# Window attention and a gated MLP on one core: 64-wide TensorE tiles for the attention, units of six blocks, and a transpose split between VectorE and DMA

## The chip, the core and the metric

The kernel runs on one core of one Trainium2 chip. A core has five engines with a queue each: TensorE (PE, matmuls; PEld is its weight load), VectorE (DVE), ScalarE (ACT), GpSimd (POOL) and SyncE (SP, which here only issues DMAs). Each engine takes its instructions in order and waits on semaphores for what other engines and the DMAs have made. The metric is the device time of one execution in microseconds (us); lower is better. The kernel before takes 1037.87 us (median of three runs, 1037.74 to 1038.93).

## The reference

`q`, `k`, `v` are (8 batches, 8 heads, 576 tokens, 64) in float32. Attention is causal with a window of 64 keys, its output becomes 4608 rows of 512, and these go through an MLP of width 2048 with a gate:

```
scores = q @ k.T / 8                     # masked unless 0 <= query - key < 64
attn   = softmax(scores)                 # over at most 64 keys
x      = (attn @ v) as [4608, 512]       # 8 heads side by side
h      = x @ w_in                        # [4608, 2048]
g      = h * tanh(log1p(exp(min(h, 20))))   # h itself instead of the logarithm above 20
out    = g @ w_out                       # [4608, 512]
```

The two weight matrices are handed to the chip as float64 bits; the kernel splits each into a high and a low float32r part there.

## The kernel before, in words

**Layout.** Heads go in four pairs, so that a pair fills 128 partitions (two heads of 64 channels). Tokens go in 12 chunks of 384, a chunk in six blocks of 64 queries. A block of queries sees two blocks of keys, its own and the one ahead of it, hence 128 keys. There are 288 such (pair, block) items in all, 24 a chunk.

**Attention of one block** (L126 to L173), in groups of three blocks. `q_t` holds the two heads of a pair apart in the columns, with zeros across the heads, so one 128x128x128 float32 matmul (L126) gives both heads' scores `s_ps`. VectorE adds the mask and takes the row minimum of the negated scores (L131). ScalarE takes the exponential and its row sum (L135). VectorE adds 1e-9 and inverts the sum (L137, L138). GpSimd multiplies the rows by it for the first three chunks; later VectorE does two blocks of three (L143) and GpSimd one (L141). The product `pr` has queries on partitions and must be transposed to `pT`, keys on partitions. Chunks 0 and 1 do that with TensorE (L157) and a ScalarE copy (L158). From chunk 2 on VectorE does it in 32x32 squares (L153): ten instructions a group, of 32x96 each, without the squares that the mask empties. Then `o_ps` is one 128x128x128 float32 matmul a block (L165), of which only the two diagonal quarters are used: ScalarE rounds them to float32r as `xh` (L172), VectorE takes the rest as `xl` (L173). Each float32 matmul is two LDWEIGHTS and two MATMUL records in the trace.

**MLP of one chunk**: 16 steps `f`. A step is twelve matmuls of 384 columns into `h_ps` (L181: three products of high and low parts, four slices of 128 channels), then the gate, and nine matmuls of 512 columns into three accumulators `acc` (L211). The gate is exp on ScalarE (L188), a clip on VectorE (L193), square, logarithm and exp on ScalarE (L194 to L196), a product on VectorE (L198), and the split in `gh` and `gl` on GpSimd (L199, L200). The matmuls into `acc` run two steps behind those into `h_ps` (`LAG`). Where no attention runs beside (`alone`), ScalarE first copies `h_ps` to `h` (L192).

**Weights.** 32 pieces of 512 columns are loaded once and split by bit operations (`load_w`, L225 to L245): four or five VectorE instructions a piece (L236 to L243), ScalarE rounds (L244), and VectorE or GpSimd subtracts (L245). `take_w(2)` asks for two pieces a step.

**Order of the work.** First the attention of chunks 0 and 1, with eight pieces of weights between. Then a segment `both` of 24 steps: all 16 of chunk 1 and the first eight of chunk 0, while the other pieces are split. Then the last eight steps of chunk 0 beside the attention of chunk 2. From there on chunk c's 16 steps stand beside the attention of chunk c+1; chunk 11 has none beside it. `Att.plan` gives each group's three stages (scores, transpose, values) a slot among the half steps. A scheduler then fixes each engine's order; a tile is taken from a pool with a fixed number of buffers, in the program's order, and an instruction that needs a buffer waits for whoever last used it. Before the change the gate's `t` has four buffers of its own, and the split's `wa` has two of its own.

Of the kernel before, what the change touches and what calls it, by code (L numbers as in the profile page):

```python
# [19 lines left out]
BLK = 64          # the attention window; queries and keys go in blocks of it  # L20
# [3 lines left out]
WP = 512          # columns of weights taken at a time  # L24
# [3 lines left out]
def tile_window_attn_mish_ffn(  # L28
    ctx: ExitStack,
    tc: tile.TileContext,  # L30
    q2: bass.AP,      # [pairs, 128 (head of the pair, d), blocks x (head, 64 queries)], zero across heads
    kT: bass.AP,      # [pairs, 128, 64 + tokens]
    vN: bass.AP,      # [pairs, 64 + tokens, 128]
    w_in: bass.AP,    # [f tiles, 128, c tiles, 128], the doubles' bits
    w_out: bass.AP,   # [f tiles, 128, 512], the doubles' bits
    out: bass.AP,     # [tokens, 512]
# [3 lines left out]
    NPAIR, _, NT = q2.shape  # L40
    NT //= 2
# [6 lines left out]
    G = 3                       # blocks of an attention group  # L48
    NG = NB // G
# [16 lines left out]
    mask0 = const.tile([P, P], F32, name="mask0")  # L66
# [7 lines left out]
    nc.gpsimd.tensor_copy(mask0, mask)  # L74
    nc.gpsimd.memset(mask0[:, 0:BLK], NEG)

# [5 lines left out]
    pTs = [const.tile([P, G, P], F32, name=f"pT{i}") for i in range(2)]  # L82
# [4 lines left out]
    marks = {}        # the last of VectorE's instructions on a group's scores  # L87

    def load_qk(c, p):
        q_t = ap_.tile([P, NB, P], F32, name="q_t")  # L90
        k_t = ap_.tile([P, CH + BLK], F32, name="k_t", bufs=2)
        qf = q_t.rearrange("p n s -> p (n s)")
        parts = NG if c == 0 and p < 2 else 1
        for i in range(parts):
            a, b = i * CH // parts, (i + 1) * CH // parts
            nc.sync.dma_start(qf[:, 2 * a:2 * b], q2[p, :, 2 * (c * CH + a):2 * (c * CH + b)])
            a, b = a + BLK * (i > 0), b + BLK
            nc.sync.dma_start(k_t[:, a:b], kT[p, :, c * CH + a:c * CH + b])
# [10 lines left out]
    def att_scores(c, i, tiles):  # L109
        p, g = units[i]  # L110
        q_t, k_t = tiles
        if c < 2:
            n = i % NTT
            s_ps = ps_acc.tile([P, G, P], F32, name="s_ps", tag=f"acc{n}")
        else:
            s_ps = ps_at.tile([P, G, P], F32, name="s_ps", tag="at")
        if c < 2 and i % 2 == 0:
            # the tiles of the gate, which has not begun
            pr = mp.tile([P, CH], F32, name="prt", tag="t", bufs=4).rearrange("p (g s) -> p g s", g=G)
        else:  # L120
            pr = ap_.tile([P, G, P], F32, name="pr", bufs=3)
        mx = ap_.tile([P, G], F32, name="mx", bufs=5)
        sm = ap_.tile([P, G], F32, name="sm", bufs=5)
        for j in range(G):
            n = g * G + j
            nc.tensor.matmul(s_ps[:, j, :], q_t[:, n, :], k_t[:, n * BLK:n * BLK + P],  # L126
                             start=True, stop=True)
        for j in range(G):
            first = (c * NB + g * G + j) % blocks_per_seq == 0
            # -(scores + mask) / 8 and its minimum, which is minus the maximum  # L130
            marks[c, i] = nc.vector.tensor_tensor_reduce(  # L131
# [283 lines left out]
```

## Time and profile before

| what | value |
|---|---|
| runs | 1037.87, 1038.93, 1037.74 us |
| profiled execution: span | 1039.1 us (its time outside the span is not recorded apart) |
| mean granted TensorE clock | 0.982 |
| busy: PE / PEld / DVE / ACT / POOL | 979.3 / 877.7 / 796.2 / 625.8 / 398.9 us |
| end of the attention of chunks 0 and 1, first gate on DVE | 63.1 us |
| chunk 1's first result leaves on DVE | 186.6 us |
| chunk 2's first full step on PE | 249.7 us |
| a chunk from 3 to 9 | 80 us each |
| DMA | 76.05 MB, 73 GB/s over the span |

PE's busy time is near the span, but matmul ends are modelled and a waiting matmul counts as busy, so PE is read by the starts of its instructions: the distance from one start to the next. The stages differ, so they are read one by one.

### The profile page before, as it was taken

How to read it: one execution, taken by the hardware profiler on the slowest of the kernel's cores; microseconds unless marked ns; L12 is line 12 of the kernel's file. 1: busy time of each engine (PE TensorE's matmuls, PEld its weight loads, DVE VectorE, ACT ScalarE, POOL GpSimd, SP SyncE). 2: the span in 40 equal slices, each digit the busy share in tenths (PEclk: the TensorE clock that was granted, in tenths of full speed). 3: DMA queues.
4: the chain of work that ended last, by engine and by line, in shares of the span. 5: the costliest groups of instructions: out<-in, count | busy, mean ns of one | idle time of the engine just before them, and what ended most of it. 6: DMA issues, size and time to landing. Idle time of an engine off the chain costs nothing.

```text
span 1039.1 us, 16752 instructions
## 1 busy us (share of the span) xinstructions
PE 979.3 (94%) x5232; PEld 877.7 (84%) x5232; DVE 796.2 (77%) x2621; ACT 625.8 (60%) x1668; POOL 398.9 (38%) x583
## 2 busy tenths in 40 slices
PE   7689887977989999999999999999999999999998
PEld 6687776876979988898889898888988889888887
DVE  4899997798778778777787877877877887885332
ACT  6765776555656655665656565655665655655664
POOL 5645555432333332433334233343333333333432
PEclk9889999988999999999999999999999999999999
DMA  8743441232211211211311211221221211200000
GB/s 264 237 136 110 132 124 41 82 93 77 73 55 50 85 55 41 94 51 45 94 41 56 76 58 55 71 64 40 85 64 40 85 42 62 84 3 1 31 1 31
DMA packets 61913, 76.05 MB, mean 73 GB/s; under 512 B 3456, under 2 KB 47232, under 8 KB 61824
## 3 DMA queue, kind: packets, MB, share of 16 engines
q1 hardware_dynamic: 57936, 60.83, 18.8%
q0 software_dynamic: 3888, 14.16, 4.5%
q8 instruction: 41, 0.67, 0.3%
q14 instruction: 48, 0.39, 0.1%
HBM read 65.54 MB, written 9.44 MB: 72 GB/s over the span
## 4 chain that ended last, share of the span: by engine, by line
PE 49%; DVE 34%; ACT 10%; issue 4%; DMA 2%; POOL 1%; SPq 0%; ACTq 0%; DVEq 0%; POOLq 0%
PE h_ps L181 21%; PE acc L211 21%; DVE pT L153 13%; ACT pr L135 4%; PE o_ps L165 3%; PE s_ps L126 3%; DVE t L193 3%; DVE pr L143 3%; DVE t L198 2%; DVE wa L242 2%; DVE xl L173 2%; DVE sm L137 2%; DVE wa L243 2%; ACT t L194 1%; ACT t L195 1%
## 5 line engine op out<-in xcount | busy, mean ns | idle before, releaser
L199 POOL TENSOR_SCALAR gh<-t 128x384 fp32r<-128x384 f32 x192 | 104.1, 542 | 518.9 <-DVE t L198 374.9
L181 PE MATMUL h_ps<-xh,wi_h 128*128 128x384 f32 x768 | 275.3, 359 | 9.4 <-ACT h L192 7.4
L153 DVE STREAM_TRANSPOSE pT<-pr 32x96 f32<-32x96 f32 x960 | 258.4, 269 | 14.3 <-DVE pr L143 0.5
L181 PE MATMUL h_ps<-xl,wi_h 128*128 128x384 f32 x768 | 261.5, 340 | 1.5 <-DVE xl L173 1.4
L181 PE MATMUL h_ps<-xh,wi_l 128*128 128x384 f32 x768 | 260.9, 340 | 0.8 <-POOL wi_l L245 0.8
L194 ACT ACTIVATE t<-t 128x384 f32<-128x384 f32 x192 | 100.8, 525 | 232.3 <-DVE t L193 232.0
L211 PE MATMUL acc<-wo_h,gh 128*128 128x512 f32 x576 | 231.1, 401 | 5.5 <-POOL gh L199 5.5
L211 PE MATMUL acc<-wo_l,gh 128*128 128x512 f32 x576 | 228.0, 396 | 0.0
L211 PE MATMUL acc<-wo_h,gl 128*128 128x512 f32 x576 | 216.4, 396 | 0.0
L200 POOL TENSOR_TENSOR gl<-t,gh 128x384 fp32r<-128x384 f32 x192 | 199.9, 1041 | 15.6
L181 PEld LDWEIGHTS h_ps<-xh,wi_h 128*128 128x128 f32 x768 | 146.9, 191 | 17.9 <-ACT h L192 10.7
L181 PEld LDWEIGHTS h_ps<-xl,wi_h 128*128 128x128 f32 x768 | 147.2, 192 | 4.1 <-DVE xl L173 2.1
L181 PEld LDWEIGHTS h_ps<-xh,wi_l 128*128 128x128 f32 x768 | 146.5, 191 | 2.0 <-POOL wi_l L245 1.5
L198 DVE SCALAR_TENSOR_TENSOR t<-t,h_ps 128x384 f32<-128x384 f32 x152 | 83.8, 551 | 79.7 <-ACT t L196 77.4
L211 PEld LDWEIGHTS acc<-wo_h,gl 128*128 128x128 f32 x576 | 108.0, 188 | 26.6 <-POOL gl L200 1.0
L211 PEld LDWEIGHTS acc<-wo_h,gh 128*128 128x128 f32 x576 | 108.6, 189 | 25.8 <-POOL gh L199 8.3
L211 PEld LDWEIGHTS acc<-wo_l,gh 128*128 128x128 f32 x576 | 108.7, 189 | 17.6
L195 ACT ACTIVATE t<-t,half_b 128x384 f32<-128x384 f32 x192 | 118.3, 617 | 5.2
L135 ACT ACTIVATE pr<-pr,mx 128x128 f32<-128x128 f32 x264 | 102.6, 390 | 25.0 <-DVE mx L131 24.8
L165 PE MATMUL o_ps<-pT,v_t 128*128 128x128 f32 x576 | 92.4, 288 | 25.1 <-DVE pT L153 19.1
L193 DVE TENSOR_SCALAR t<-t 128x384 f32<-128x384 f32 x192 | 95.8, 500 | 25.5 <-ACT t L188 23.7
L165 PEld LDWEIGHTS o_ps<-pT,v_t 128*128 128x128 f32 x576 | 81.0, 198 | 39.1 <-DVE pT L153 18.5
(54 smaller groups left out, 1106.2 us busy)
## 6 DMA issues: line engine op xcount, KB each, us to landing
v_t<-vN SPq DMA_DIRECT2D x48, 384.0 KB, 3.5
q_t<-q SPq DMA_DIRECT2D x46, 384.0 KB, 3.3
k_t<-kT SPq DMA_DIRECT2D x46, 224.0 KB, 3.5
out<-o SPq DMA_DIRECT2D x36, 256.0 KB, 2.1
st<-w_out POOLq DMA_DIRECT2D x14, 512.0 KB, 4.0
st<-w_in POOLq DMA_DIRECT2D x13, 512.0 KB, 4.0
st<-w_in SPq DMA_DIRECT2D x3, 512.0 KB, 5.9
st<-w_out SPq DMA_DIRECT2D x2, 512.0 KB, 4.6
```

The source lines that it names most:

```text
L126: nc.tensor.matmul(s_ps[:, j, :], q_t[:, n, :], k_t[:, n * BLK:n * BLK + P], start=True, stop=True)
L135: nc.scalar.activation(pr[:, j, :], pr[:, j, :], AF.Exp, bias=mx[:, j:j + 1], scale=-1.0, accum_out=sm[:, j:j + 1])
L153: nc.vector.transpose(pT[k:k + 32, :, r:r + 32], pr[r:r + 32, :, k:k + 32])
L165: nc.tensor.matmul(o_ps[:, j, :], v_t[:, g * G + j, :], pT[:, j, :], start=True, stop=True)
L181: nc.tensor.matmul(h_ps, w[:, f, cc, :], xx[:, cc, :], start=n == 0, stop=n == 3 * NC_ - 1)
L193: nc.vector.tensor_scalar(t, t, EXP20, 1.0, ALU.min, ALU.add)
L194: nc.scalar.activation(t, t, AF.Square)
L195: nc.scalar.activation(t, t, AF.Ln, bias=half_b, scale=0.5)
L198: nc.vector.scalar_tensor_tensor(t, t, -1.0, h, ALU.add, ALU.mult)
L199: nc.gpsimd.tensor_scalar(gh, t, 1.0, 0.0, ALU.mult, ALU.add)
L200: nc.gpsimd.tensor_tensor(gl, t, gh.bitcast(F32), ALU.subtract)
L211: nc.tensor.matmul(acc[t], a[:, ts_], w[:, f, :], start=f == 0 and i == 0, stop=f == NF - 1 and i == 2)
```

## The change

1. `q_t` no longer has the zeros across the heads (half the bytes). Scores are made with 64x64 tiles of TensorE: contraction 64 (one head's channels), 64 queries, 128 keys. A unit is now all six blocks of a pair in a chunk; its 12 score matmuls go to four tiles in turn, and partitions hold (parity of the block, 64 queries) with the head along the free dimension.
2. `o_ps` is made per head and block: contraction over 128 keys, 64 channels, 64 queries; 12 matmuls a unit. `xh` and `xl` are then one instruction each for 128x384.
3. All products with the inverted sum are GpSimd's.
4. From chunk 2 on the transpose is one VectorE instruction of 128x768 into a tile `tr`, in 32x32 squares within the partitions, and twelve SBUF-to-SBUF DMAs on SP, of 32 partitions and 192 floats each, that carry the squares to their partitions in `pT`.
5. `pr` and `tr` share two buffers; `wa` takes its buffers from the gate's `t`, four for both. The `h` of the steps without attention has two buffers instead of three.
6. Four units a chunk stand at `plan`'s slots 0, 6, 12, 18, with the transpose 3.6 and the values 6 half steps after the scores.

The core of the diff:

```diff
-    pTs = [const.tile([P, G, P], F32, name=f"pT{i}") for i in range(2)]
+    pTs = [const.tile([P, P // 32, HM, 32], F32, name=f"pT{i}") for i in range(2)]
...
+        pr = ap_.tile([P, HM, P], F32, name="pr", bufs=2)
...
-        for j in range(G):
-            n = g * G + j
-            nc.tensor.matmul(s_ps[:, j, :], q_t[:, n, :], k_t[:, n * BLK:n * BLK + P],
-                             start=True, stop=True)
+        for m in range(NM):
+            for par, h in ((0, 0), (1, 1), (1, 0), (0, 1)):
+                n = 2 * m + par
+                rows = slice(h * BLK, (h + 1) * BLK)
+                nc.tensor.matmul(s_ps[h][par * BLK:(par + 1) * BLK, m, :],
+                                 q_t[rows, n * BLK:(n + 1) * BLK], k_t[rows, n * BLK:n * BLK + P],
+                                 start=True, stop=True)
...
+        for j in range(HM):
+            nc.gpsimd.tensor_scalar(pr[:, j, :], pr[:, j, :], sm[:, j:j + 1], 0.0, ALU.mult, ALU.add)
...
+            tr = ap_.tile([P, P // 32, HM, 32], F32, name="tr", tag="pr", bufs=2)
+            nc.vector.transpose(tr.rearrange("p k j i -> p j k i"),
+                                pr.rearrange("p j (k i) -> p j k i", i=32))
             for r in range(0, P, 32):
                 for k in range(0, P, 32):
                     if 0 <= k - r % BLK <= BLK:
-                        nc.vector.transpose(pT[k:k + 32, :, r:r + 32], pr[r:r + 32, :, k:k + 32])
+                        nc.sync.dma_start(pT[k:k + 32, r // 32, :, :], tr[r:r + 32, k // 32, :, :])
...
+        for n in range(NB):
+            m, par = n // 2, n % 2
+            for h in range(2):
+                rows = slice(h * BLK, (h + 1) * BLK)
+                nc.tensor.matmul(o_ps[rows, n * BLK:(n + 1) * BLK], v_t[:, n, rows],
+                                 pT[:, 2 * par:2 * par + 2, h * NM + m, :], start=True, stop=True)
+        nc.scalar.copy(xh[:, p, :], o_ps)
+        nc.vector.tensor_tensor(xl[:, p, :], o_ps, xh[:, p, :].bitcast(F32), ALU.subtract)
...
-        a = mp.tile([P, WP], U32, name="wa")
+        a = mp.tile([P, WP], U32, name="wa", tag="t", bufs=4)
...
+            step = (slots - 2) / (NPAIR + 1)
+            for p in range(NPAIR):
+                at = p * step
+                self.events += [(at, 2, self.scores, p), (at + 0.6 * step, 1, self.transpose, p),
+                                (at + step, 0, self.values, p)]
```

**What moved, on DVE, near the end of `both`.** Before, two of the last steps of that segment (L193 and L198 are the gate, L239 to L243 the split of a piece of weights into `wa`):

```order
L239 TENSOR_SCALAR wa_1371<-wa_1371 128x512
L198 SCALAR_TENSOR_TENSOR t_1717<-t_1717,h_1721 128x384
L241 TENSOR_SCALAR wa_1371<-wa_1371 128x512
L242 SCALAR_TENSOR_TENSOR wa_1371<-st_1369,wa_1371 128x512
L193 TENSOR_SCALAR t_1752<-t_1752 128x384
L243 SCALAR_TENSOR_TENSOR wa_1371<-st_1369,wa_1371 128x512
L239 TENSOR_SCALAR wa_1381<-wa_1381 128x512
L241 TENSOR_SCALAR wa_1381<-wa_1381 128x512
L242 SCALAR_TENSOR_TENSOR wa_1381<-st_1379,wa_1381 128x512
L198 SCALAR_TENSOR_TENSOR t_1752<-t_1752,h_1756 128x384
L243 SCALAR_TENSOR_TENSOR wa_1381<-st_1379,wa_1381 128x512
L193 TENSOR_SCALAR t_1787<-t_1787 128x384
```

The same steps of the changed kernel (there L200 and L205 are the gate):

```order
L205 SCALAR_TENSOR_TENSOR t_1720<-t_1720,h_1724 128x384
L200 TENSOR_SCALAR t_1755<-t_1755 128x384
L205 SCALAR_TENSOR_TENSOR t_1755<-t_1755,h_1759 128x384
L200 TENSOR_SCALAR t_1790<-t_1790 128x384
L205 SCALAR_TENSOR_TENSOR t_1790<-t_1790,h_1794 128x384
```

Before, one piece goes with each step up to the last of the 24. Now, with `t` and `wa` in one ring, pieces go two a step in the program's order: eight are done ahead of the first step, 31 ahead of the 13th, and the last eleven steps have none.

**What moved, on PE, in a late chunk.** Before, three blocks' values and two blocks' scores stand between two steps of the MLP:

```order
L211 MATMUL acc_6937<-wo_l,gh 128x512
L211 MATMUL acc_6937<-wo_h,gl 128x512
L165 MATMUL o_ps<-pT_104,v_t 128x128 x3
L126 MATMUL s_ps<-k_t,q_t 128x128 x2
L181 MATMUL h_ps<-xh_5892,wi_h 128x384
```

Now:

```order
L188 MATMUL h_ps<-xl_6526,wi_h 128x384
L177 MATMUL o_ps<-pT_107,v_t 64x64 x2
L126 MATMUL s_ps<-k_t,q_t 64x128 x12
L188 MATMUL h_ps<-xh_6525,wi_l 128x384
L218 MATMUL acc_7523<-wo_h,gh 128x512
L218 MATMUL acc_7523<-wo_l,gh 128x512
L218 MATMUL acc_7523<-wo_h,gl 128x512
L218 MATMUL acc_7524<-wo_h,gh 128x512
L177 MATMUL o_ps<-pT_107,v_t 64x64 x10
L218 MATMUL acc_7524<-wo_l,gh 128x512
```

A unit's scores stand right behind the first two value matmuls of the unit ahead of it, which wait for six of its DMAs; the other ten wait for all twelve. PE goes five times a unit from one shape of tile to another.

**What moved, on SP, in a late chunk.** Now:

```order
L157 DMA pT_107<-tr 32x192 x12
L99 DMA q_t<-qT 128x384
L101 DMA k_t<-kT 128x448
L108 DMA v_t<-vN 128x6x128
L157 DMA pT_106<-tr 32x192 x12
L99 DMA q_t<-qT 128x384
L101 DMA k_t<-kT 128x448
L108 DMA v_t<-vN 128x6x128
```

Before, the same stretch of the queue holds the three loads of a pair and a chunk's three stores, and nothing that VectorE or PE waits for within a unit. A unit's loads now stand behind its twelve DMAs.

More of the change, by code (lines that the diff above doesn't have):

```diff
@@ new lines, in att_scores @@
+        for m in range(NM):
+            first = [(c * NB + 2 * m + par) % blocks_per_seq == 0 for par in range(2)]
+            mk = firsts[first.index(True)] if any(first) else mask
+            for h in range(2):
+                j = h * NM + m
+                marks[c, p] = nc.vector.tensor_tensor_reduce(
+                    out=pr[:, j, :], in0=s_ps[h][:, m, :], in1=mk,
+                    op0=ALU.add, op1=ALU.min, scale=-0.125, scalar=3.0e38, accum_out=mx[:, j:j + 1])
+                nc.scalar.activation(pr[:, j, :], pr[:, j, :], AF.Exp, bias=mx[:, j:j + 1], scale=-1.0,
+                                     accum_out=sm[:, j:j + 1])
@@ L345, in tile_window_attn_mish_ffn @@
     ev = []
-    for u in range(2 * NU):
-        a, i = first[u // NU], u % NU
-        ev += [(u, 2, a.scores, i), (u + 1.5, 1, a.transpose, i), (u + 2.25, 0, a.values, i)]
+    for u in range(2 * NPAIR):
+        a, p = first[u // NPAIR], u % NPAIR
+        ev += [(u, 2, a.scores, p), (u + 0.75, 1, a.transpose, p), (u + 1.25, 0, a.values, p)]
     for _, _, fn, i in sorted(ev, key=lambda e: e[:2]):
```

124 lines of the change are left out of this document (44 added, 80 removed).

## The prediction

> **What bounds the kernel now.** I read first the page's busy times and chain, then busy time by stage, then waits and single instructions of each stage. No one engine bounds the whole:
>
> ```profile
> PE   979.3 (94%) x5232; PEld 877.7 (84%) x5232; DVE 796.2 (77%) x2621; ACT 625.8 (60%) x1668; POOL 398.9 (38%) x583
> PE 49%; DVE 34%; ACT 10%; issue 4%; DMA 2%; POOL 1%; SPq 0%; ACTq 0%; DVEq 0%; POOLq 0%
> ```
>
> The chain of waits runs half through PE and a third through DVE. By stage (busy us of PE, PEld, DVE, ACT, POOL):
>
> ```profile
> 63.00:178.00 115.00, 101.43 (x474) 85.55 (x474) 111.37 (x174) 77.53 (x157) 66.35 (x75) 0.98 0.35 106
> 187.00:250.00 63.00, 50.91 (x277) 45.52 (x276) 54.18 (x230) 34.42 (x112) 20.47 (x41) 0.90 0.31 100
> 250.00:335.00 85.00, 81.65 (x438) 73.67 (x437) 67.57 (x257) 47.50 (x134) 27.52 (x41) 0.97 0.18 54
> 495.00:575.00 80.00, 79.17 (x434) 71.64 (x433) 63.46 (x226) 47.70 (x131) 27.86 (x40) 1.00 0.20 62
> 970.00:1039.00 69.00, 64.44 (x319) 57.06 (x317) 20.52 (x32) 39.20 (x78) 24.54 (x31) 0.98 0.06 24
> ```
>
> While weights are split (63 to 178) DVE is the bound, 97% busy. Beside the attention of chunk 2 (187 to 250) PE idles and its clock falls to 0.90. From chunk 3 on a chunk takes 80 us and PE is the bound, DVE has 16 us to spare. In chunk 11, without attention, a step of the MLP takes PE 4.19 us (994.51 less 990.32 below), a chunk 67 us:
>
> ```profile
> 990.32 2.10 PE acc L211 x9
> 992.42 2.08 PE h_ps L181 x12
> 994.51 2.10 PE acc L211 x9
> ```
>
> So attention costs PE 13 us of the 80. Its price a matmul record:
>
> ```profile
> 505.62 0.38 PE L126 MATMUL s_ps<-k_t,q_t 128*128 128x128 f32 x2
> 505.84 0.83 PE L165 MATMUL o_ps<-pT,v_t 128*128 128x128 f32 x6
> ```
>
> From start to start (505.84 - 505.62) / 2 = 0.110 us; six take 0.83, which is five times 0.111 and a last one of 0.275. A record thus holds PE 0.111 and has a tail of 0.165 that the next hides. A chunk has 96 such records, 10.6 us; 2.4 us are left for waits:
>
> ```profile
> PE o_ps L165 <- DVE pT L153: 1.3, 3, 0.7
> ```
>
> (480 to 560 us; us in all, times, longest.) The transposes thus cost PE little here, though they cost DVE most:
>
> ```profile
> L153 DVE STREAM_TRANSPOSE pT<-pr 32x96 f32<-32x96 f32 x960 | 258.4, 269 | 14.3 <-DVE pr L143 0.5
> ```
>
> Taking 258 us from DVE is worth something only between 187 and 335.
>
> **The change part by part.** The sum goes against the profiled execution, span 1039.1; its time outside the span is not given, and the median of the runs, 1037.9, is 1.2 lower, so 1.2 comes off at the end.
>
> *1. Start to the end of chunk 1.* Before, chunk 1's first result leaves at 186.6, and DVE has its last piece of weights behind it at 178:
>
> ```profile
> 178.12 1.15 DVE L193 TENSOR_SCALAR t<-t 128x384 f32<-128x384 f32 x2 [2.06 <-ACT t L188]
> 186.61 0.69 DVE L220 TENSOR_SCALAR o<-acc 128x512 f32<-128x512 f32 x1 [0.64 <-PE acc L211]
> ```
>
> The new order splits two pieces a step: all are done by the 13th step, and eleven steps follow in which DVE has only the gate. The steps' matmuls, hidden under DVE before, then stand alone: 11 times 2.08 (h_ps) and 13 times 2.10 (acc, two steps behind) = 50 us. Ahead of them DVE has 24 pieces and 12 gates. Price now: 111.4 busy for 25 pieces and 23 gates; a gate 0.50 + 0.55 by the groups:
>
> ```profile
> L193 DVE TENSOR_SCALAR t<-t 128x384 f32<-128x384 f32 x192 | 95.8, 500 | 25.5 <-ACT t L188 23.7
> L198 DVE SCALAR_TENSOR_TENSOR t<-t,h_ps 128x384 f32<-128x384 f32 x152 | 83.8, 551 | 79.7 <-ACT t L196 77.4
> ```
>
> leaves (111.4 - 24.2) / 25 = 3.5 us a piece. That is a crowded price, with POOL at work over half the time; the same instruction is short or long:
>
> ```profile
> 65.55 0.68 DVE L242 SCALAR_TENSOR_TENSOR wa<-st,wa 128x512 uint32<-128x512 uint32 x1
> 66.15 0.41 DVE L239 TENSOR_SCALAR wa<-wa 128x512 f32<-128x512 f32 x1
> 66.49 0.68 DVE L243 SCALAR_TENSOR_TENSOR wa<-st,wa 128x512 uint32<-128x512 uint32 x1
> 67.09 0.35 DVE L193 TENSOR_SCALAR t<-t 128x384 f32<-128x384 f32 x1
> 138.76 1.25 DVE L239 TENSOR_SCALAR wa<-wa 128x512 f32<-128x512 f32 x1
> ```
>
> By the starts, undisturbed, L242 and L243 take 0.60 each and L239 0.34; with L241 like L239 and L245 like L243 a piece is 2.5. Bounds of the split: 24 x 3.5 + 12 x 1.05 = 97, and 24 x 2.5 + 12 x 0.75 = 69. POOL has half as many gates to split in that stretch, which speaks for the lower end; one ring of four for `t` and `wa` adds waits, which speaks for the upper. I take 87. The attention of chunks 0 and 1 ends at 60 for 63 (half the bytes of q; DVE has eight `xl` for sixteen). 60 + 87 + 50 = 197: **+10** (-8 to +20).
>
> *2. Beside chunk 2's attention* (186.6 to 249.7, 63 us). A unit's scores stand on PE behind the first values of the unit ahead, so four units run one behind another, and the unit's own chain sets the pace:
>
> ```profile
> 506.98 0.29 DVE L131 CUSTOM_DVE_ANT_0 pr<-s_ps,mask 128x128 f32<-128x128 f32 x1
> 508.62 0.39 ACT L135 ACTIVATE pr<-pr,mx 128x128 f32<-128x128 f32 x1
> 509.00 0.39 ACT L135 ACTIVATE pr<-pr,mx 128x128 f32<-128x128 f32 x1
> L137 DVE TENSOR_SCALAR sm<-sm 128x3 f32<-128x3 f32 x96 | 29.1, 304 | 36.5 <-ACT pr L135 35.6
> L138 DVE RECIPROCAL sm<-sm 128x3 f32<-128x3 f32 x96 | 16.6, 174 | 2.8
> L141 POOL TENSOR_SCALAR pr<-pr,sm 128x128 f32<-128x128 f32 x120 | 49.4, 418 | 38.5 <-DVE sm L138 26.6 <-DVE sm L137 5.7 <-ACT t L188 2.7
> 15.28 0.33 SPq L96 DMA_DIRECT2D q_t<-q  x1
> 15.71 0.39 SPq L98 DMA_DIRECT2D k_t<-kT  x1
> out<-o SPq DMA_DIRECT2D x36, 256.0 KB, 2.1
> ```
>
> First scores and minimum 0.5; six exponentials 0.38 apart and one gate instruction between, 2.8; sum and inverse 0.5; POOL's rest of a split 0.5, six products 2.5; DVE's rest 0.5; the transpose. For 128x768 no row exists: by elements from 0.27 for 96 it would be 2.2, by two passes like L193 1.0; the bulk of 0.27 for so few elements must be fixed, so 1.1. SP issues 0.43 apart at most, 0.40 with the lengths 0.33 to 0.39 and a gap: six are 2.4, and landing is 2.1 by the nearest row (256 KB to HBM; 24 KB within SBUF should not be slower). Together 12.9 us from a unit's scores to its sixth DMA, 15.3 to its twelfth. Four units: 3 x 12.9 + 15.3 = 54; 4.2 from the end of chunk 1 to the first scores, 1.6 for the last values, `xh` and `xl`; less 1.6 of chunk 2's first matmuls that the order puts between units. 58 for 63: **-5** (-12 to +8, chains of 11 to 16).
>
> *3. Chunk 2* runs 249.7 to 335.3 with DVE 79% busy; freed of transposes it should keep the later chunks' 80: **-6** (-6 to 0).
>
> *4. Attention on PE, 36 units beside nine chunks.* Before, 24 records of 0.111 a unit, 2.66 us. Now 24 score records (128 columns on a 64x64 tile) and 24 value records (64 columns). No row has a tile below 128x128. Bounds: if tiles take turns, 24 x 0.111 + 24 x 0.056 = 4.0; if four score tiles and two value tiles ran wholly side by side, 0.67 + 0.67 = 1.3. Between: the two records of one matmul share a tile and must follow each other, while the second can run beside the next matmul's first. Then a matmul costs one record: 12 x 0.111 + 12 x 0.056 = 2.0. To this comes the price of changing shape, five times a unit: nothing, or the tail of 0.165 that the next record can no longer hide, at most with a weight load laid open too (PEld mean 0.198):
>
> ```profile
> L165 PEld LDWEIGHTS o_ps<-pT,v_t 128*128 128x128 f32 x576 | 81.0, 198 | 39.1 <-DVE pT L153 18.5 <-issue 11.2 <-PE acc L211 4.6
> ```
>
> I take the tail, 0.83 a unit: 2.83 for 2.66, 36 x 0.17 = **+6** (-48 to +78).
>
> The Trainium skill, TensorEngine Tiling (Array Packing), Key Properties, says that changing the tiling mode drains TensorE; by that rule the tail is paid, without it term 4 is -24. No trace here can show it: all matmuls of this kernel have one shape. The same skill's TensorE: Matmul & The Clock Gate, Part 3, has tiles of different positions start about 4 ns apart; that bears on the overlap, and again no row here does.
>
> *5. DMAs in the steady chunks.* From a unit's scores to the values that wait for them PE has 15.3 us of other work by the order (three steps and more), to the last ten 17.5; the chains are 12.9 and 15.3. Hidden, **0**, by 2.4 us; without that cover each us costs 36, since behind the waiting values PE holds the next unit's scores and an MLP step, and DVE's minima, the gate and `acc` wait for these. On DVE the transpose waits for POOL's last product; behind it stands the gate's L205 of one step, which has two steps (8.4 us) until `acc` needs it: 0. Each DMA also waits until the eighth ahead of it has landed: 8 x 0.40 = 3.2 against 2.1, no wait. The loads of the next pairs stand behind the twelve on SP; they are due a unit (20 us) later.
>
> Costing nothing: the products on POOL, 24 x 0.418 = 10 us a chunk where 8 were POOL's before, beside 28 busy of 80; the freed DVE time (its 63 of 80 falls to some 35) waits for PE.
>
> Sum: 1039.1 + 10 - 5 - 6 + 6 - 1.2 = **1043**.
>
> **The rivals.**
> *A, faster:* tiles overlap as above and changing shape costs nothing: term 4 is -24. 1037.9 + 10 - 5 - 6 - 24 = 1013; 995 with the split at its lower end. For it: nothing in the trace shows a cost of going from 384 to 128 columns. Against: there the tile stays the same. The price decides: 180 changes of p us give 1013 + 180 p, faster than before below p = 0.13.
> *B, slower:* the tiles take turns, through the shared weights' path or because the change does not place them apart: 4.0 a unit, 36 x 1.34 = +48, and 0 to 30 for the changes: 1085 to 1115, 1100. For it: before, a record of 0.111 never began inside another.
> *C, slower:* the DMAs come late. Stores have landed as late as 5.5:
>
> ```profile
> DMA to landing us min/median/max: 2.0/2.1/5.5
> ```
>
> With 3.4 us more, less the cover of 2.4, every unit waits 1 us: +36, 1079.
>
> **How the numbers follow.** Forecast 0.40 (1025 to 1062 alone), A 0.27, B 0.22, C 0.11. A difference under 0.2%, 2 us, is what a measurement here cannot tell from none. A is faster, B and C slower; the forecast's own range lies a third below 1036 and half above 1040. Faster 0.27 + 0.40 x 0.3 = 0.39, same 0.05, slower 0.56. Eight in ten: the lower third of A (0.1) and the upper half of B (0.1) left out, 1008 to 1108.
>
> **What would show it.** Starts of `s_ps` records 0.055 apart in the mean (overlap) or 0.11 (turns); a gap of some 0.17 at each change of shape; DVE idle in the last third of `both`, chunk 1's result near 197; four units of 13 us for chunk 2; no PE wait on DMA from chunk 3 on; chunks of 80 to 81 us. Wrong it would be if chunks came under 78 or over 84, or if the eleven bare steps ran under the split after all.

## The result, and the profile after

The changed kernel takes 1051.8 us in the median (1050.85 to 1052.23), the kernel before, timed beside it, 1038.3: a ratio of 1.0124 (95% interval 1.0109 to 1.0138). The forecast was 1043, slower by 0.5%. The sign is right and the time lies in the range, but the loss is two and a half times the forecast's, and it is the small remainder of large terms, three of which were wrong. The profiled execution took 1050.85 us, its span is 1049.1.

The page of the changed kernel, busy times and chain of waits:

```profile
PE 963.9 (92%) x6384; PEld 825.5 (79%) x6384; DVE 460.3 (44%) x1317; ACT 600.4 (57%) x1524; POOL 444.4 (42%) x729
PE 81%; DVE 8%; DMA 3%; ACT 3%; issue 2%; SPq 2%; POOL 1%; ACTq 0%; DVEq 0%; POOLq 0%
```

DVE lost 336 us of work, and its share of the chain fell from 34% to 8%. PE's rose from 49% to 81%. Where the time went shows only by stage. First two stages of the kernel before, the split of the weights and what follows it to chunk 1's first result (columns: stretch, its length, then busy us of PE, PEld, DVE, ACT and POOL, granted clock, DMA share, GB/s):

```profile
63.10:176.10 113.00, 99.43 (x464) 83.64 (x463) 111.27 (x174) 76.51 (x155) 64.53 (x73) 0.98 0.36 108
176.10:186.20 10.10, 9.49 (x50) 8.44 (x49) 3.74 (x6) 6.92 (x15) 5.79 (x8) 1.00 0.00 0
```

And the stages of the changed kernel: start to first gate, first gate to the last piece of weights, from there to chunk 1's first result, from there to chunk 2's last `xl`, chunk 2, a steady chunk:

```profile
0.00:74.90 74.90, 46.84 (x456) 33.74 (x456) 40.14 (x164) 35.90 (x132) 35.67 (x78) 0.79 0.59 188
74.90:164.40 89.50, 62.75 (x260) 52.45 (x261) 87.58 (x143) 54.99 (x107) 45.29 (x50) 0.90 0.38 124
164.40:213.10 48.70, 48.70 (x243) 43.69 (x242) 16.68 (x26) 29.17 (x60) 21.48 (x27) 1.00 0.00 1
213.10:281.10 68.00, 48.28 (x384) 40.28 (x382) 22.17 (x93) 30.03 (x95) 19.94 (x40) 0.79 0.30 90
281.10:363.80 82.70, 79.54 (x529) 68.80 (x528) 30.32 (x100) 47.31 (x121) 33.56 (x57) 0.94 0.21 60
517.80:594.50 76.70, 76.70 (x530) 66.39 (x530) 30.79 (x97) 45.48 (x119) 34.51 (x61) 1.00 0.23 69
```

| stage, us | before | forecast | changed |
|---|---|---|---|
| start to first gate | 63.1 | 60 | 74.9 |
| first gate to last piece | 113.0 | 87 | 89.5 |
| to chunk 1's first result | 10.1 | 50 | 48.7 |
| to chunk 2's last `xl` | 63.3 | 58 | 68.0 |
| chunk 2 | 85.8 | 80 | 82.7 |
| chunks 3 to 11 | 703.8 | 710 | 685.3 |

(The forecast's last row is 703.8 with its term 4, +6.) Against the kernel before, the first three rows give +26.9, the next two +4.7 and -3.1, the last -18.5: +10.0, the difference of the spans. The split does leave PE alone behind it: DVE is 98% busy in one row and 34% in the next, PE 70% and 100%. And a steady chunk takes 76.7 us where it took 80.0, with PE busy throughout.

What a unit of attention now costs PE, from the timeline of PE in a steady chunk (start, length, instruction, records):

```profile
529.21 0.34 PE L188 MATMUL h_ps<-xl,wi_h 128*128 128x384 f32 x1
529.48 0.34 PE L177 MATMUL o_ps<-pT,v_t 128*64 128x64 f32 x4
529.74 0.89 PE L126 MATMUL s_ps<-k_t,q_t 64*64 64x128 f32 x24
530.56 0.44 PE L188 MATMUL h_ps<-xh,wi_l 128*128 128x384 f32 x1
530.84 0.39 PE L218 MATMUL acc<-wo_h,gh 128*128 128x512 f32 x1
531.30 0.39 PE L218 MATMUL acc<-wo_h,gl 128*128 128x512 f32 x1
531.62 0.80 PE L177 MATMUL o_ps<-pT,v_t 128*64 128x64 f32 x20
532.35 0.51 PE L218 MATMUL acc<-wo_h,gh 128*128 128x512 f32 x1
532.69 0.39 PE L218 MATMUL acc<-wo_l,gh 128*128 128x512 f32 x1
```

An undisturbed `h_ps` record follows the last by 0.176 (ten from 527.45 to 529.21), an `acc` record by 0.233 (2.10 us for nine). From 529.21 to 530.84 are 1.63, two `h_ps` in it: 1.28 for the attention. From 531.30 to 532.69 are 1.39, two `acc` in it: 0.93. This unit costs 2.2 us, with five changes of shape; in the mean of the five chunks from 517.8 to 902.8 a unit has 5.6 changes and costs 2.3, because some units are split further. Before, it was 24 records of 0.111, 2.66; the forecast said 2.83.

The records are not all that a chunk lost. Before, values also waited for VectorE's transposes:

```profile
515.17 0.61 PE L126 MATMUL s_ps<-k_t,q_t 128*128 128x128 f32 x4
516.08 0.71 PE L165 MATMUL o_ps<-pT,v_t 128*128 128x128 f32 x4 [0.30 <-DVE pT L153]
```

Four records of 0.111 take 0.44, and from start to start they took 0.91: 0.47 are lost where the profile's view of waits counts 0.30, because it counts from the modelled end of the record ahead. By the starts, with 0.111 taken off for every record, the kernel before lost 11.4 us so in the five chunks from 494.5 to 894.8, 2.3 a chunk; the waits view has 4.8, 1.0 a chunk.

The new operations of transposing, first DVE's, then SP's DMAs (least, median and longest ns, and the DMAs' us to landing):

```profile
L152 DVE STREAM_TRANSPOSE tr<-pr x40: 958/978/980, 224.9 to 954.2; 128x768 f32<-128x768 f32 x40
L157 SPq DMA_DIRECT2D pT<-tr x480: 507/588/1647, 225.9 to 962.8; - x160
DMA to landing us min/median/max: 1.7/1.8/4.1
```

### The profile page after: what moved, and what is told of

Same layout as the page of the kernel before. It is cut to its first block, busy times and chain, and to the rows that moved or that the text cites. A ratio compares the mean times of both kernels' runs of the same rounds, so it can differ in the third digit from the quotient of the medians.

```text
span 1049.1 us, 18496 instructions
## 1 busy us (share of the span) xinstructions
PE 963.9 (92%) x6384; PEld 825.5 (79%) x6384; DVE 460.3 (44%) x1317; ACT 600.4 (57%) x1524; POOL 444.4 (42%) x729
## 4 chain that ended last, share of the span: by engine, by line
PE 81%; DVE 8%; DMA 3%; ACT 3%; issue 2%; SPq 2%; POOL 1%; ACTq 0%; DVEq 0%; POOLq 0%
PE h_ps L188 38%; PE acc L218 35%; PE o_ps L177 4%; PE s_ps L126 4%; DMA st<-w_out 1%; ACT pr L138 1%; DVE wa L249 1%; SPq L157 1%; DVE wa L250 1%; DVE wa L248 1%; DVE wa L246 1%; POOL pr L143 1%; DVE t L205 1%; DVE pr L135 1%; DVE tr L152 1%
## 5 line engine op out<-in xcount | busy, mean ns | idle before, releaser
L188 PE MATMUL h_ps<-xh,wi_h 128*128 128x384 f32 x768 | 267.5, 349 | 11.1 <-DVE t L205 5.1
L188 PE MATMUL h_ps<-xh,wi_l 128*128 128x384 f32 x768 | 265.3, 345 | 0.0
L188 PE MATMUL h_ps<-xl,wi_h 128*128 128x384 f32 x768 | 265.0, 345 | 0.0
L207 POOL TENSOR_TENSOR gl<-t,gh 128x384 fp32r<-128x384 f32 x192 | 196.7, 1024 | 15.8
L218 PE MATMUL acc<-wo_h,gl 128*128 128x512 f32 x576 | 202.7, 396 | 0.0
L195 ACT ACTIVATE t<-h_ps 128x384 f32<-128x384 f32 x192 | 93.9, 489 | 188.5 <-PE h_ps L188 152.7
L200 DVE TENSOR_SCALAR t<-t 128x384 f32<-128x384 f32 x192 | 107.2, 558 | 161.9 <-ACT t L195 161.9
L143 POOL TENSOR_SCALAR pr<-pr,sm 128x128 f32<-128x128 f32 x288 | 107.2, 391 | 144.0 <-DVE sm L141 130.3
L205 DVE SCALAR_TENSOR_TENSOR t<-t,h_ps 128x384 f32<-128x384 f32 x152 | 83.5, 549 | 185.8 <-ACT t L203 185.6
L138 ACT ACTIVATE pr<-pr,mx 128x128 f32<-128x128 f32 x288 | 111.8, 390 | 85.6 <-DVE mx L135 85.6
L201 ACT ACTIVATE t<-t 128x384 f32<-128x384 f32 x192 | 100.6, 524 | 99.0 <-DVE t L200 98.4
L203 ACT ACTIVATE t<-t 128x384 f32<-128x384 f32 x192 | 100.6, 524 | 5.2
```

The source lines that it names most:

```text
L138: nc.scalar.activation(pr[:, j, :], pr[:, j, :], AF.Exp, bias=mx[:, j:j + 1], scale=-1.0, accum_out=sm[:, j:j + 1])
L143: nc.gpsimd.tensor_scalar(pr[:, j, :], pr[:, j, :], sm[:, j:j + 1], 0.0, ALU.mult, ALU.add)
L188: nc.tensor.matmul(h_ps, w[:, f, cc, :], xx[:, cc, :], start=n == 0, stop=n == 3 * NC_ - 1)
L195: nc.scalar.activation(t, h_ps, AF.Exp)
L200: nc.vector.tensor_scalar(t, t, EXP20, 1.0, ALU.min, ALU.add)
L201: nc.scalar.activation(t, t, AF.Square)
```

## The experiments

Ratios are to the kernel before, which ran beside each of them at 1038.3 to 1039.3 us.

| kernel | us | ratio, 95% interval |
|---|---|---|
| changed | 1051.8 | 1.0124, 1.0109 to 1.0138 |
| e1, `wa` in buffers of its own | 1035.9 | 0.9973, 0.9958 to 0.9989 |
| e2, later transposes at the start | 1048.4 | 1.0085, 1.0065 to 1.0106 |
| e3, chunk 2 transposed on PE | 1031.5 | 0.9929, 0.9910 to 0.9948 |
| e4, scores tile by tile | 1091.1 | 1.0509, 1.0488 to 1.0530 |
| e5, VectorE's 32x32 transposes | 1057.2 | 1.0175, 1.0148 to 1.0201 |
| e6, e1 + e2 + e3 | 1010.3 | 0.9720, 0.9692 to 0.9749 |
| e7, e2 with two early pieces | 1049.3 | 1.0102, 1.0072 to 1.0131 |
| e8, values in one run | 1113.8 | 1.0715, 1.0695 to 1.0734 |
| e9, e6 with values in one run | 1058.2 | 1.0182, 1.0153 to 1.0212 |
| e10, e5 with values in one run | 1061.6 | 1.0216, 1.0196 to 1.0236 |
| e11, before with the shared ring | 1064.0 | 1.0241, 1.0222 to 1.0260 |
| e12, chunk 2's DMAs on two queues | 1050.4 | 1.0119, 1.0086 to 1.0152 |

### The ring that `wa` and `t` share (e1, e11)

```diff
-        a = mp.tile([P, WP], U32, name="wa", tag="t", bufs=4)
+        if i < 8:
+            a = mp.tile([P, WP], U32, name="wa", tag="t", bufs=4)
+        else:
+            a = ap_.tile([P, WP], U32, name="wa", tag="v_t", bufs=2)
```

> The changed kernel, but from the ninth piece of weights on `wa` takes two buffers of its own (those of `v_t`, idle in that stage) instead of turns in the ring of four with the gate's `t`. Reference: changed kernel 1051.8. Theory (the shared ring holds the gates back): in the changed kernel DVE does 24 pieces and 12 gates in 86 us (74.9 to 161.0), then 11 bare steps take 52 us, 4.7 a step. Now DVE's order has 18 or 19 gates among the pieces and 5 behind them: 86 + 7 x 1.05 = 93, then 5 x 4.7 = 24: chunk 1's first store at 192 for 213.3, total about 1030. Rival (the pieces and the late start set the stage, whoever owns the buffers): the more gates among the pieces only lengthen DVE's stretch, store at 210 to 213, total 1049 to 1052.

(The expectation counts the split to the thirteenth gate, at 161.0; its last instruction ends at 164.4.) Measured, 1.5% less than the changed kernel, about 16 us; VectorE takes chunk 1's first result at 194.9 for 213.3. The same two stages as above, of e1:

```profile
72.60:177.50 104.90, 91.59 (x428) 77.53 (x428) 96.57 (x154) 71.30 (x144) 62.45 (x65) 0.97 0.31 106
177.50:194.50 17.00, 15.14 (x75) 13.02 (x74) 6.67 (x11) 10.67 (x22) 8.32 (x11) 1.00 0.15 45
```

The bare stretch shrinks from 48.7 to 17.0, the split grows from 89.5 to 104.9, in which PE now does 92 us of work for 63. Before the last piece is done 21 of the 24 gates have begun, 14 in the changed kernel. All later stages keep their lengths. Then the same ring put into the kernel before, nothing else:

```diff
-        t = mp.tile([P, CH], F32, name="t", bufs=4)
+        t = mp.tile([P, CH], F32, name="t", tag="t", bufs=4)
...
-        a = mp.tile([P, WP], U32, name="wa")
+        a = mp.tile([P, WP], U32, name="wa", tag="t", bufs=4)
```

> The kernel before with one part of the change alone: `wa` takes its turns in the ring of four with the gate's `t`; attention, tiles and transposes are the old ones. Theory (the ring alone puts eleven gates behind the split): DVE's order has 13 to 14 gates up to the last piece and 11 behind it, as in the changed kernel; chunk 1's first store moves from 186 to 203 to 210, total 1054 to 1062, ratio 1.016 to 1.022, since giving `wa` its own buffers took 16 to 18 us off the changed kernel. Rival (the ring costs only together with units of six blocks and their later start): under 5 us, total 1038 to 1043.

1064.0, +25 us: more than expected. Its trace was taken at a granted clock of 0.56 and gives VectorE's order, not the times: the last piece's last bit step (L243, at 164.6) stands behind the 14th gate (L193, at 163.3), as in the changed kernel, where the kernel before has 23 gates ahead of its last. So the ring alone, without units of six blocks and without new tiles, puts the gates behind the split, and it costs more than the whole change did. In that kernel the attention of chunks 0 and 1 also uses tiles of `t`; how much of the 25 that is stays open. A ring with more than four buffers was not run, so the runs do not tell the order that the ring imposes from its small number of buffers.

### The start (e2, e7)

```diff
-        ev += [(u, 2, a.scores, p), (u + 0.75, 1, a.transpose, p), (u + 1.25, 0, a.values, p)]
+        ev += [(u, 2, a.scores, p), (u + 1.25, 1, a.transpose, p), (u + 1.75, 0, a.values, p)]
```

> The changed kernel with one line other: in the attention of chunks 0 and 1 a unit's PE transposes and values stand half a unit later, behind the next unit's scores. Theory (PE's order makes the start one serial chain: scores, minima, exponentials, products, transposes, and only then the next scores): two units overlap, the first gate on DVE moves from 74.9 to 60 to 64, nothing behind it changes, total 1038 to 1042. Rival (the start waits for loads of k and for the weights' DVE work, or the two buffers of `pr` hold the next unit back anyway): first gate at 73 to 76, total 1049 to 1053.

The theory fell: the first gate moves only from 74.9 to 72.7 (rows below), the time by some 4 us. The next run took six of the pieces of weights out of the start instead.

```diff
-    for u in (2, 4, 5, 5, 6, 7, 7, 7):
+    for u in (2, 4):
```

> The kernel of the later transposes with only two of the eight pieces of weights split in the attention of chunks 0 and 1; the other six follow beside the MLP. It asks why that attention ends at 72.7 to 74.9 and not at the 60 of the forecast. Theory (the pieces do it: DVE's sums and inverses of the last units stand in its order behind pieces that wait for their weights): first gate at 58 to 63, the split longer by six pieces of 3 us, so chunk 1's first store later by 3 to 8 us than 211, total 1050 to 1058. Rival (the chain of eight units and the loads of k, each waiting for the scores two units ahead): first gate at 68 to 73 still, store at 220 or later, total 1058 to 1068.

First gate of the changed kernel, of e2 and of e7, from VectorE's timelines:

```profile
74.91 0.36 DVE L200 TENSOR_SCALAR t<-t 128x384 f32<-128x384 f32 x1 [1.81 <-ACT t L195]
```
```profile
72.75 0.36 DVE L200 TENSOR_SCALAR t<-t 128x384 f32<-128x384 f32 x1 [1.35 <-ACT t L195]
```
```profile
58.28 0.36 DVE L200 TENSOR_SCALAR t<-t 128x384 f32<-128x384 f32 x1 [1.30 <-ACT t L195]
```

So the chain of eight units alone ends near 58, and six pieces hold it up by 14. How, the changed kernel's own rows show, for a unit whose sum (L140) and inverse (L141) stand in VectorE's order among the steps of two pieces:

```profile
56.23 1.48 DVE L243 TENSOR_SCALAR wa<-st 128x512 uint32<-128x512 uint32 x1
58.97 0.16 DVE L140 TENSOR_SCALAR sm<-sm 128x6 f32<-128x6 f32 x1
59.04 0.68 DVE L249 SCALAR_TENSOR_TENSOR wa<-st,wa 128x512 uint32<-128x512 uint32 x1
60.71 0.18 DVE L141 RECIPROCAL sm<-sm 128x6 f32<-128x6 f32 x1
```

POOL's six products and PE's transposes wait for L141. But the 14 us are not a loss of their own: in e7 the pieces come back in the split, which ends at 173.4; chunk 1's first result leaves at 209.3, earlier than expected, and the total is that of e2 within the intervals.

### Beside chunk 2's attention (e3, e12)

```diff
-        if c >= 2:
+        if c >= 3:
             tr = ap_.tile([P, P // 32, HM, 32], F32, name="tr", tag="pr", bufs=2)
```

> The changed kernel, but chunk 2's attention transposes on PE with ACT's copies as chunks 0 and 1 do; from chunk 3 on the DMAs stay. Theory (the DMA chain sets the pace of chunk 2's four units: transpose 1.0, six issues of SP at 0.63, 1.8 to land, the twelfth 3.8 later): a unit then has six PE transposes and two ACT copies, about 2.5 us, for 6.6, and no second half: scores of units 9 to 10 us apart for 13.5, the stage from chunk 1's store to chunk 2's x 48 to 50 us for 68, total 1032 to 1036. Rival (the units are serial by PE's order, and the PE transposes now wait there for POOL's products with the MLP's matmuls queued behind): the stage shortens by under 5 us, total 1047 to 1052.

The time falls by 2.0% of the changed kernel, about 20 us. The two stages of e3 that answer to 213.10:281.10 and 281.10:363.80:

```profile
214.20:255.90 41.70, 37.70 (x352) 30.04 (x351) 14.26 (x71) 26.37 (x84) 16.35 (x34) 1.00 0.29 90
255.90:343.70 87.80, 87.80 (x586) 75.89 (x585) 33.78 (x118) 53.90 (x142) 37.01 (x62) 1.00 0.24 70
```

Scores of one unit and the next stand 6.6 to 11.4 us apart for 13.1 to 16.9. The stage is even shorter than the theory had it, since the order, made anew, left more of chunk 0's MLP for later: chunk 0's first result moves from 247.3 to 267.3, and chunk 2 takes 5 us more. Is it the issuing of the DMAs? e12 halves it:

```diff
-                        nc.sync.dma_start(pT[k:k + 32, r // 32, :, :], tr[r:r + 32, k // 32, :, :])
+                        eng = nc.scalar if c == 2 and (r // 32) % 2 else nc.sync
+                        eng.dma_start(pT[k:k + 32, r // 32, :, :], tr[r:r + 32, k // 32, :, :])
```

> The changed kernel, but the six DMAs of the rows 32 to 63 and 96 to 127 of chunk 2's transposed tiles are issued by ACT, the other six by SP; so the first values wait for three issues of either queue, not for six of one. Theory (in the chain of 13.5 us a unit the issues at 0.63 us are what the forecast priced too low, at 0.40): three issues less, 1.9 us a unit, and the last values 3.8 earlier: scores 11.5 to 12 us apart, the stage 60 to 63 us for 68, total 1043 to 1047. Rival (ACT's six issues, 3.6 us a unit, push its exponentials and the gate back by as much): stage 66 to 70, total 1050 to 1055.

The theory fell: 1050.4, the stage 66.6 us. PE's waits between 213 and 282, first of the changed kernel, then of e12 (us in all, times, longest):

```profile
PE o_ps L177 <- DMA pT<-tr: 18.0, 6, 6.0
```
```profile
PE o_ps L178 <- DMA pT<-tr: 8.0, 2, 4.6
PE h_ps L189 <- DVE t L206: 5.3, 1, 5.3
PE h_ps L189 <- ACT xh L180: 4.0, 2, 2.0
```

The wait for the DMAs is smaller, and waits for the gate and for `xh` (1.7 us in the changed kernel) stand in its place; chunk 0's first result moves from 247.3 to 259.6, so its MLP steps now run between the units. As these rows read, the stage is two serial chains, the unit's and the gate's, on one ordered PE, and earlier DMAs alone only changed which one PE waits for.

### Side by side, or one after another (e4)

```diff
-        for m in range(NM):
-            for par, h in ((0, 0), (1, 1), (1, 0), (0, 1)):
+        for par, h in ((0, 0), (1, 1), (1, 0), (0, 1)):
+            for m in range(NM):
```

> The changed kernel with the score matmuls in another order: the three of one 64x64 tile one behind the other, then the next tile, instead of the four tiles in turn. Theory (the gain of the steady chunks comes from four tiles at work side by side: 24 records start 0.027 us apart): records of one tile follow each other 0.107 apart, 20 x 0.107 + 3 x 0.027 = 2.2 a unit for 0.62, 36 units: +57, total 1100 to 1112, a steady chunk 83 for 76.9. Rival (a 64x64 matmul is cheap by itself, whatever stands beside it): pitch stays 0.027, total 1050 to 1054. Between: two tiles overlap, 0.054, +23.

+39 us on the changed kernel, a mean steady chunk 80.3 for 77.0. The scores of one unit in e4:

```profile
554.12 1.69 PE L126 MATMUL s_ps<-k_t,q_t 64*64 64x128 f32 x24
555.74 0.45 PE L188 MATMUL h_ps<-xh,wi_l 128*128 128x384 f32 x1
```

From the first to the next MLP record 1.62 for 0.82: the order alone doubles their price. It is the case between that the expectation names: 23 starts in 1.42 us (1.62 less the 0.20 that the change takes behind the last), 0.062 apart, so some two tiles still overlap. That the matmul is cheap by itself is excluded. Some 8 us of the 39 are the later start, 82.7 for 74.9.

### What the DMAs are worth in the steady chunks (e5)

```diff
-            tr = ap_.tile([P, P // 32, HM, 32], F32, name="tr", tag="pr", bufs=2)
-            nc.vector.transpose(tr.rearrange("p k j i -> p j k i"),
-                                pr.rearrange("p j (k i) -> p j k i", i=32))
...
-                        nc.sync.dma_start(pT[k:k + 32, r // 32, :, :], tr[r:r + 32, k // 32, :, :])
+                        nc.vector.transpose(pT[k:k + 32, r // 32, :, :], pr[r:r + 32, :, k:k + 32])
```

> The changed kernel with the one 128x768 transpose and the twelve DMAs undone: VectorE makes the twelve 32x32 transposes (32x192 each) straight into `pT`, from chunk 2 on; units and 64-wide tiles stay. Theory (the DMA chain costs only beside chunk 2's attention, and from chunk 3 on it is hidden and takes a wait off PE): in the unit's chain 12 x 0.3 to 0.35 = 4 us stand for 1.0 + 6 x 0.63 + 1.8 = 6.6, pace there 10.5 to 11 for 13.5, -10 to -14 us; a steady chunk rises by the waits of PE on DVE's `pT`, 0.5 to 1.2 of the 2.4 us that the kernel before had, 77.4 to 78.1: +4 to +10; total 1041 to 1050. Rival 1 (from chunk 3 on the transposes cost nothing wherever they stand): chunk 76.9, total 1036 to 1041. Rival 2 (DVE's time is what the change frees and PE gets): chunks 79 and more, total over 1058.

+5 us on the changed kernel: the chunk 2 stage is 12 us shorter (269.5 - 213.9 = 55.6 for 68.0), but a steady chunk is 1.7 us longer. One of the chunks, the transposes, and one unit on PE:

```profile
516.40:595.00 78.60, 78.60 (x529) 66.94 (x528) 43.23 (x141) 45.22 (x118) 33.23 (x56) 1.00 0.17 53
```
```profile
L154 DVE STREAM_TRANSPOSE pT<-pr x480: 358/370/377, 225.8 to 960.0; 32x192 f32<-32x192 f32 x160
```
```profile
549.67 0.34 PE L174 MATMUL o_ps<-pT,v_t 128*64 128x64 f32 x4
549.93 0.86 PE L126 MATMUL s_ps<-k_t,q_t 64*64 64x128 f32 x18
550.73 0.45 PE L174 MATMUL o_ps<-pT,v_t 128*64 128x64 f32 x6
551.10 0.45 PE L185 MATMUL h_ps<-xh,wi_h 128*128 128x384 f32 x1
553.39 0.68 PE L174 MATMUL o_ps<-pT,v_t 128*64 128x64 f32 x14
554.00 0.44 PE L126 MATMUL s_ps<-k_t,q_t 64*64 64x128 f32 x6
554.37 0.50 PE L215 MATMUL acc<-wo_h,gh 128*128 128x512 f32 x1
```

DVE is busy 55% and PE waits for nothing: PE is full in this row, and the waits view of the five chunks from 516.4 is empty. So the kernel before's waits for VectorE's transposes do not need the DMAs to go; they are gone here too. PE works longer because the values and scores of a unit fall into more runs, seven changes here for five above, in the mean 7.8 for 5.6. So the DMAs' gain in the steady chunks is not the time that they take off DVE. It comes with an order in which fewer changes of shape stand: at 0.17 a change (next section) 8.6 changes a chunk are 1.5 of the 1.7 us.

### The price of a change of shape (e8, e9, e10)

```diff
-        for n in range(NB):
+        for n in (1, 0, 3, 2, 5, 4):
             m, par = n // 2, n % 2
```

> The changed kernel with the blocks of a unit's values in the order 1, 0, 3, 2, 5, 4: the first of them then needs all twelve DMAs, and the order on PE becomes one run of 24 value records and one of 24 score records, 3.1 changes between MLP, scores and values a unit for 5.8. It asks what a change of tile shape costs. Theory (a change costs PE about 0.2 us: the kernel with VectorE's transposes has 7.8 to 8.0 changes a unit and 0.445 us more PE time a unit, 0.208 a change; the forecast took 0.165): 2.65 x 0.165 to 0.208 = 0.44 to 0.55 us a unit, a steady chunk 74.7 to 75.2 for 76.9. Beside chunk 2's attention each unit waits 3.8 us longer, +11 to +15. Total 1043 to 1050. Rival (changes are free, the extra PE time is waits): chunk 76.5 to 77, total 1062 to 1068.

> The three cures together (1010) with the blocks of the values in the order 1, 0, 3, 2, 5, 4 as well; chunk 2's attention goes over PE here, so nothing waits for twelve DMAs there. Theory (0.165 to 0.208 us a change): 36 units x 0.44 to 0.55 = -16 to -20, total 990 to 995, steady chunk 74.7 to 75.2. Rival (changes are free): 1008 to 1013.

> The kernel with VectorE's twelve 32x32 transposes (1057, chunk 78.7) with the same order of the values: 5.0 changes a unit for 8.0. Theory (its chunks are longer than those with DMAs only for its 2.1 changes more a unit, not for VectorE's 4.4 us a unit): 3.0 x 0.165 to 0.208 = 0.49 to 0.62 a unit, chunk 76.2 to 76.7 as with DMAs or below, total 1034 to 1040. Rival (VectorE's transposes themselves hold PE): chunk 78 and more, total 1052 to 1058.

The totals went against all three expectations: +62, +48 and +4 us on the changed kernel, on e6 and on e5, where less time was expected (the +4 lies within the intervals). The price itself came out as expected. One unit of e9 in a steady chunk:

```profile
509.95 0.63 PE L218 MATMUL acc<-wo_h,gl 128*128 128x512 f32 x2
510.51 0.92 PE L177 MATMUL o_ps<-pT,v_t 128*64 128x64 f32 x24
511.36 0.89 PE L126 MATMUL s_ps<-k_t,q_t 64*64 64x128 f32 x24
512.18 0.50 PE L218 MATMUL acc<-wo_h,gh 128*128 128x512 f32 x1
512.51 0.39 PE L218 MATMUL acc<-wo_l,gh 128*128 128x512 f32 x1
```

From 510.18 (the second of the two `acc`, 0.233 behind the first) to 512.51 are 2.33, less two `acc` 1.86. With three changes a unit costs 1.86, with five 2.2: 0.17 a change, and 1.36 for the 48 records without any. (In the five chunks of the changed kernel, 20 units with 112 changes cost 46.4 us by the starts; 20 x 1.36 + 112 x 0.17 is 46.2.) That is four score tiles and two value tiles wholly side by side. Nor were the changes free, as the rival had it. What the totals missed is in PE's waits of e9 between 500 and 900 us:

```profile
PE h_ps L188 <- DVE t L205: 21.3, 4, 5.3
```

Once a chunk PE now stands still for 5.3 us. The last unit's values, which wait for all twelve DMAs, come so late that the next chunk's first steps lack a quarter of `x`: both banks of `h_ps` are held by steps that have 9 of their 12 records, and when the values are there and these two are complete, PE waits for the first gate. On the chain this gate stands behind the next unit's twelve exponentials on ScalarE (2.4 us), since that unit's scores follow the values on PE. The chain of waits of e9 at such a boundary, up to the values:

```profile
566.83 1.59 PE h_ps L188 x9
568.42 2.10 PE acc L218 x9
570.52 0.87 PE o_ps L177 x24
```

A mean chunk is 82.8 us for the 77.0 of e6. In e10 the same wait is 7.1 us in all over the same stretch, and the mean chunk falls only to 78.4 from 78.7. So the split of the values into 4 and 20 records, which costs two changes a unit, pays for itself.

### The three cures together (e6)

The edits of e1, e2 and e3.

> The changed kernel with three cures together: `wa` in buffers of its own from the ninth piece on, the start's transposes half a unit later, PE transposes in chunk 2's attention. One by one they gave -16, -4 and -21 against the changed kernel (1052 on this scale of before = 1038 to 1039). Theory (three stages one behind another, so the gains add): -41, total 1009 to 1014, ratio to the kernel before 0.971 to 0.977. Rival (what is saved in the split is waited for again beside chunk 2's attention, since that stage then starts earlier against the same loads): total 1018 to 1028.

The gains add: 1010.3 us, 2.8% faster than the kernel before and 4.0% faster than the changed one. Its first gate is at 68.7, chunk 1's first result at 190.6, chunk 2's last `xl` at 233.4, and chunk 2 ends at 321.1, where the changed kernel has 74.9, 213.1, 281.1 and 363.8.

The new tiles are worth their steady chunks; what the change lost, it lost in the first 280 us, through two decisions that the tiles don't need.

## Why the prediction was right in sign and wrong in size

**Term 1, +10 forecast, +26.9 measured; the step that failed is "the attention of chunks 0 and 1 ends at 60".** The two other parts of that sum held: 87 for the split was 89.5, 50 for the bare steps was 48.7. The 60 was the old start less 3. But 24 pieces in the split mean eight in the start, and the sum gave them no time: it took for granted that they hide beside the attention, as seven had done before (six whole, and the seventh's bit steps) in 63.1 us. In the new order they hold up the units. e7 shows both sides: with two pieces the start ends at 58.3, with eight at 72.7 in e2. The mechanism, that with the shared ring PE's last steps stand alone, is shown by e1 and again by e11.

**Term 2, -5 forecast, +4.7 measured; the step that failed is "four units run one behind another, and the unit's own chain sets the pace".** It holds for all intervals but the first. Between the scores of one unit and the next are 16.9, 13.7, 13.1 and 13.7 (the last up to chunk 3's first unit), for 12.9. In the first interval the sixth DMA lands at 230.9, but PE, in its order, works at the MLP until 234.6; so the three intervals inside the stage are 43.7 for 38.7. From the last unit's scores to its last `xl` are 19.4, for 16.9 less the 1.6 of MLP that the forecast took off, and the stage's first scores come 0.6 later than forecast: 5.0 + 4.1 + 0.6 = 9.7, the whole miss. SP's issues were mis-sized, 0.63 apart for 0.40, but landing is 1.8 for 2.1: the sixth DMA lands 4.9 after the first issue for 4.5, the twelfth 8.7 for 6.9. e12 shows that the right issue price would not have repaired the sum: with half the issues on a queue the stage is 66.6 for 68.0.

**Term 3, -6 forecast, -3.1 measured.** Chunk 2 took 82.7, not 80, at a mean clock of 0.94; in it PE waits once 3.2 us for a gate.

**Term 4, +6 forecast, -18.5 measured over chunks 3 to 11; two steps failed, "a matmul costs one record" and the 2.4 us a chunk left for waits.** The forecast set the overlap at half of what it is. The records cost 1.36 a unit, the lower bound that it had worked out (1.3) and not taken; the price of a change, 0.165, was right (0.17 by e9), and the changes are 5.6 in the mean for five. 1.36 + 5.6 x 0.17 = 2.3. Of the 3.1 us that a steady chunk lost (80.1 to 77.0, the mean of five), 4 x (2.66 - 2.3) = 1.4 are this. The rest is the waits that the forecast read off as 80 - 67 - 10.6 and left standing: 2.3 us a chunk before by the starts, 0.3 now (two waits for a gate in the five chunks, 1.1 us in all in the waits view, 1.5 by the starts). The two parts make 3.4, so the account closes within 0.3. e5 shows that these waits go without the DMAs too, with the units of six blocks and their new order; which of the two takes them away is not shown. Chunks 10 and 11 together are 2.0 us longer (146.3 for 144.3), which is not explained.

The Trainium skill, TensorE: Matmul & The Clock Gate, Part 3, gives a pack of tiles the time of one matmul and about 4 ns for each further tile. An estimate by that page is 0.12 for four score records (0.111 + 3 x 0.004). The trace agrees: 24 records starting within 0.62 us are 0.11 for four; the records of one group start 6 to 7 ns apart in it, not 4. That rule, which the prediction cited for the starts alone, would have led to its lower bound. The Trainium skill, TensorEngine Tiling (Array Packing), Key Properties, says that a change of tiling mode drains TensorE; the 0.17 a change agrees with it.

**Term 5, 0 forecast.** Right: from chunk 3 on PE waits for no DMA. e8 and e9 show how thin the cover is: if the first values also wait for the twelfth DMA, the chunk boundary opens by 5.3 us.

**The rivals.** A, tiles overlap and changes are free, was right in its first half; the price that was to decide came out at 0.17, above its limit of 0.13 for a gain, and yet term 4 is a gain, since the limit was worked out with the forecast's overlap. B is excluded by the score starts 0.027 apart, which e4 undoes by the order alone; C by the absent waits. Terms 1 to 3 erred by 30 us one way and term 4 by 24 the other; that is why the total came within 9 us of the forecast, which is luck, not sizing. Of the 9, the stages make 5; the other 4 are the step from the span to the median, forecast as -1.2 and measured as +2.7 (1049.1 to 1051.8).

**What was to show it.** Score starts 0.055 apart in the mean: they are 0.027. A gap of some 0.17 at each change: so. DVE idle in the last third of `both`: 34% busy there. Chunk 1's result near 197: 213. Four units of 13 us: 13.1 to 16.9. No wait for DMAs from chunk 3: so. Chunks of 80 to 81: 76.7, under the 78 that was named as the sign of a wrong forecast.

## What to carry to other kernels

Two tiles that share a small ring of buffers had their instructions put in the order of the program: look at what the ring orders before counting the bytes it saves. Price small matmuls on different parts of the array as a group, one record's time for as many tiles as stand next to each other, and count the changes of shape separately; the order of the matmuls decides both. Read waits on PE from start to start; the waits view counts less. When work is moved ahead of a stage, the stage ahead has to pay for it in the sum.

## What the hardware showed that was not expected

Four 64x64 tiles ran at full overlap, two records to a matmul: 24 score records in 0.62 us of starts, in turn, and 1.42 when ordered tile by tile. A DMA of 24 KB between places of SBUF held SP for 0.59 us, the loads of q and k quoted in the prediction 0.33 and 0.39. VectorE's transpose of 128x768 took 0.98, twelve of 32x192 0.37 each, 4.4 together, while those of 32x96 had taken 0.27 each. By these three an estimate is 0.17 us fixed and 0.10 for every 96 elements of a partition (0.27, 0.37, 0.97): the fixed part is most of the smallest and little of the largest.
